# Scores of two heads as a pair, joint sums, a third unit in float32, and weights on another queue

## The chip, the cores and the metric

The kernel runs on one core of a Trainium2 chip. The metric is the device time of one execution in microseconds. A kernel's time is the median of its runs. The trace is one execution recorded by the hardware profiler; its span runs from the first to the last instruction.

## The reference

Attention over 4 batches, 8 heads, 768 positions and head size 64, with a mask that keeps the first `n_sink` = 4 keys and the last `window` = 128 keys of each row; its output, as 3072 rows of 512, goes through a feed-forward layer of 2048 hidden columns. All in float32:

```python
scores = scale * np.matmul(q, k.transpose(0, 1, 3, 2))
keep = is_sink | in_window
scores = np.where(keep, scores, -1000000000.0)
scores = scores - np.max(scores, axis=-1, keepdims=True)
a = np.exp(scores)
a = a / (np.sum(a, axis=-1, keepdims=True) + 1e-09)
x = np.matmul(a, v)                 # heads side by side: [3072, 512]
h = x @ w_in                        # [512, 2048]
g = h * np.clip(h + 3.0, 0.0, 6.0) / 6.0
out = g @ w_out                     # [2048, 512]
```

## The kernel before

**Tiling.** The queries of a batch are cut into three units of 256 rows (u = 0, 1, 2). A unit holds four pairs of heads. The 48 pairs are numbered s: first the units u = 0 of the four batches (s = 0 to 15), then the others (s = 16 to 47). A pair needs, for each head h and each half t of 128 query rows, a block of scores of 128 or 256 keys (u = 0) or 272 (u above 0), the sinks included.

**Two arithmetics.** A float32 number is either used as it is, in a matmul on float32 operands which the trace shows as two records, or split into a rounded part and a remainder of type float32r, whose products are summed in PSUM. Which way a pair goes is decided by `plain(s)` (line 223): pairs s < NF32 with u = 0 are plain float32 (NF32 = 8, the first two units). A plain pair keeps its head's 64 rows of q and k where they were loaded (rows 0 to 63 for head 0, 64 to 127 for head 1) and scores with 64 rows (L306). A split pair goes through `B_k` and `B_q`: ScalarE makes the rounded half and VectorE the remainder (`split_parts`, L29 and L35), and eight transfers on SyncE's queue (L261, L274) lay them out as 128 rows `K` and `Q`. It also splits v (`A_v`), the transposed probabilities (`D_pt`: `ph`, `pl`), and joins two halves of its result (`E_out`: `tmp`).

**Stages of a pair.** `A_v` and `A_kq` load; `B_k`, `B_q` split and lay out; `C_score` multiplies and VectorE adds the mask and takes the extremum (L313); `C_soft` runs exp with sums on ScalarE (L335), two small VectorE instructions on the sums of one head (L337, L338), and the scaling of the blocks (`norm`, L321 or L323); `D_pt` transposes on TensorE; `E_av` multiplies by v; `E_out` writes the unit's input of the feed-forward layer.

**Order.** A loop over s issues the stages of three pairs by the string `ORDER` (line 548): C of pair s-1, E of s-2, loads of s+1, B of s, D of s-1. Each `-` is a `drain`, which issues one step of the feed-forward work in hand: half of an `ffn1` block (12 matmuls, L451) or an `ffn2` of one half (6 matmuls, L471). A unit has 34 such steps. A drain issues nothing while the weights of its step have not been issued. What is left after the last loop is drained at the end. `keep_busy` puts float32 matmuls without use (L81) on TensorE in the first loops.

**Weights.** They come as 64-bit numbers in 32 parts of 512 KB. `load_part` (L148) transfers a part into a buffer (`st`, three of them; each fourth part uses `vs`), ScalarE and VectorE turn it into float32 with two instructions each (L153, L157, L159, L161) and then split it with one each (L35, L164). `W` in the loop issues one part in loops 1 to 4 and four in loops 5 to 11 (`WN`). The transfer is issued by GpSimd. A buffer is free again when the fourth instruction has read it. All other transfers in the loops are issued by SyncE's queue, which waits in order.

The instructions of an engine stand in the order that the framework gave them when it scheduled the program by dependencies and buffers; it can differ a little from the order of the source.

Of the kernel before, what the change touches and what calls it, by code (L numbers as in the profile page):

```python
# [18 lines left out]
P = 128  # L19
SK = 16  # L20
WMAX = 128
SCALE = 0.125
BIG = 1.0e30
WARM = (10, 16, 4)
# [20 lines left out]
def attn_ffn_kernel(ctx: ExitStack, tc: tile.TileContext, qx, kx, vx, vfx, vsx, n_sink, window, w_in, w_out, out):  # L45
    nc = tc.nc
    B, NU, NP = qx.shape[0:3]
    NT, DM = out.shape
    NFP = w_in.shape[0]
    H, D, UT = 2 * NP, 64, 256  # L50
    S = NU * UT
# [5 lines left out]
    work = fast.enter_context(tc.tile_pool(name="work", bufs=2))  # L57
    ps = fast.enter_context(tc.tile_pool(name="ps", bufs=8, space=PSUM))
# [75 lines left out]
    def load_part(hi, lo, src, rows, at):  # L134

        def like(t):
            return t.rearrange("p (a b) -> p a b", a=rows)

        if not wide:
            st = like(work.tile([P, 512], F32, tag="st", name="st", bufs=3))  # L140
            nc.sync.dma_start(out=st, in_=src)
            split_parts(nc, hi, lo, st, nc.scalar, nc.vector)
            return

        tag, bufs = ("vs", 1) if at % 4 == 3 else ("st", 3)
        st = work.tile([P, 512, 2], I32, tag=tag, name="st", bufs=bufs)
        it = work.tile([P, 512], I32, tag="wt", name="wt", bufs=3)
        nc.gpsimd.dma_start(out=like(st.rearrange("p n w -> p (n w)")), in_=src.bitcast(I32))  # L148
        low, high = st[:, :, 0], st[:, :, 1]
        ft = it.bitcast(F32)  # L150


        nc.scalar.activation(out=ft, in_=high.bitcast(F32), func=AF.Abs, scale=2.0 ** -112)  # L153

        nc.scalar.activation(out=low, in_=low.bitcast(U32), func=AF.Copy, scale=2.0 ** -29 * (1 - 2.0 ** -18),  # L157
                             bias=7.5 * 2.0 ** -18 - 0.5)
        nc.vector.scalar_tensor_tensor(out=low, in0=high, scalar=-2 ** 31, in1=low,  # L159
                                       op0=ALU.bitwise_and, op1=ALU.bitwise_or)  # L160
# [56 lines left out]

    NF32 = 8  # L220
    PFE = "AA"
    XHF = "A"

    def plain(s):
        return s < NF32 and pus[s][1] == 0

# [59 lines left out]
    def cell(s, h, t, c0, c1):  # L286

        if plain(s):
            return st_[s][f"P{h}"][:, t * P + c0:t * P + c1]
        return st_[s]["P"][:, h, t, c0:c1]  # L290

    def C_score(s, h, t):
        b, u, p = pus[s]
        d = st_[s]
        i = 2 * h + t
        if i == 0:
            if not plain(s):
                d["P"] = work.tile([P, 2, 2, WP], F32, name="Pt", bufs=1)
            d["nb"], d["sm"], d["rc"] = (work.tile([P, 4], F32, name=x, bufs=3) for x in ("nb", "sm", "rc"))
        if t == 0 and plain(s):  # L300
            tag, bufs = PTAGS[(2 * s + h) % len(PTAGS)]
            d[f"P{h}"] = work.tile([P, 3 * P], F32, tag=tag, name="Ph", bufs=bufs)
        k0c, w, m = spans(u)[t]
        sp = ps.tile([P, 512], F32, tag="bank", name="sp")
        if plain(s):
            nc.tensor.matmul(out=sp[:, 0:w], lhsT=d["qr"][D * h:D * (h + 1), t * P:(t + 1) * P],  # L306
                             rhs=d["kr"][D * h:D * (h + 1), k0c:k0c + w], start=True, stop=True)
        else:
            K, Q = d["K"], d["Q"]
            for part in range(2):  # L310
                nc.tensor.matmul(out=sp[:, 0:w], lhsT=Q[:, h, t * P:(t + 1) * P],  # L311
                                 rhs=K[:, h, part, k0c:k0c + w], start=(part == 0), stop=(part == 1))
        d["min"] = nc.vector.tensor_tensor_reduce(out=cell(s, h, t, 0, w), in0=sp[:, 0:w], in1=m[:, 0:w], scale=-SCALE,  # L313
                                       scalar=3.0e38, op0=ALU.add, op1=ALU.min,
                                       accum_out=d["nb"][:, i:i + 1])

    NORM0, NORM = "DADA", "AAAA"

    def norm(e, blk, c):
        if e == "A":  # L320
            nc.scalar.mul(out=blk, in_=blk, mul=c)  # L321
        elif e == "D":
            nc.vector.tensor_scalar(out=blk, in0=blk, scalar1=c, scalar2=None, op0=ALU.mult)  # L323
        else:
            nc.gpsimd.tensor_scalar(out=blk, in0=blk, scalar1=c, scalar2=1.0, op0=ALU.mult, op1=ALU.mult)

    def C_soft(s, h):
        b, u, p = pus[s]
        d = st_[s]
        nb, sm, rc = d["nb"], d["sm"], d["rc"]  # L330
        hs = slice(2 * h, 2 * h + 2)
        live = [(0, W2), (0, W2)] if u else [(0, P), (0, 2 * P)]
        for t in range(2):
            i, blk = 2 * h + t, cell(s, h, t, *live[t])
            d["exp"] = nc.scalar.activation(out=blk, in_=blk, func=AF.Exp, scale=-1.0,  # L335
                                            bias=nb[:, i:i + 1], accum_out=sm[:, i:i + 1])
        nc.vector.tensor_scalar(out=sm[:, hs], in0=sm[:, hs], scalar1=1e-9, scalar2=None, op0=ALU.add)  # L337
        nc.vector.reciprocal(out=rc[:, hs], in_=sm[:, hs])  # L338
        for t in range(2):
            i, blk = 2 * h + t, cell(s, h, t, *live[t])  # L340
            norm((NORM0 if s < START else NORM)[i], blk, rc[:, i:i + 1])
        if u and h == 1:

            ss = ssc[:, :, 0:4 * SK].rearrange("p t (k h y) -> p t k h y", k=2, h=2)
            snk_in = d["P"].rearrange("p h t w -> p h (t w)")[:, :, 2 * P:2 * WP].rearrange(
                "p h (t y) -> p t h y", t=2)[:, :, :, 0:SK]
            split_parts(nc, ss[:, :, 0], ss[:, :, 1], snk_in, weng(SSE, 0), weng(SSE, 1))
# [178 lines left out]
    B_k(0)  # L526
    B_q(0)

    def slot_C(s, h, t):
        if 0 <= s < NS:  # L530
            C_score(s, h, t)
            if t == 1:
                C_soft(s, h)
                if s == 0 and h == 1:
                    keep_busy(WARM[1])
                elif 0 < s < NP:
                    keep_busy(WARM[2])

    def slot_E(s, h):
        if 0 <= s < NS:  # L540
            E_av(s, h)
# [3 lines left out]
                dsts = [out[r0 + P * tt:r0 + P * (tt + 1), :] for tt in range(2)]  # L545
                queues.append(ffn_steps(units.index((b, u)), xt[(b, u)], work, ps, ps, dsts, "bank"))

    ORDER = "V C00 - C01 E0 - C10 - C11 E1 L - Bk - Bq W - D0 - S D1 -"
    MULT = [1] * 12
    WN = [0, 1, 1, 1, 1, 4, 4, 4, 4, 4, 4, 4]  # L550

    for s in range(NS + 2):
        if s == 3:
            later_constants()
        for step in ORDER.split():
            if step == "-":
                drain(MULT[s] if s < len(MULT) else 1)
            elif step[0] == "C":
                slot_C(s - 1, int(step[1]), int(step[2]))
            elif step[0] == "E":  # L560
                slot_E(s - 2, int(step[1]))
            elif step == "V":
                if s < NS:
                    A_v(s)
                if 2 <= s and pus[s - 2][1:] == (1, 0):
                    batch_loads(pus[s - 2][0])
            elif step == "L" and s + 1 < NS and s > 0:
                A_kq(s + 1)
            elif step == "Bk" and 0 < s < NS:
                B_k(s)  # L570
            elif step == "Bq" and 0 < s < NS:
                B_q(s)
            elif step == "W":
                for _ in range(WN[s] if s < len(WN) else 0):
                    with ExitStack() as behind:
                        if s <= 5:
                            at = max(min(s, NP) - 2, 0)
                            behind.enter_context(tc.issue_after(st_[at]["min"].ins))
                            behind.enter_context(tc.issue_after(st_[at]["exp"].ins))
                        w_order.pop(0)()  # L580
            elif step[0] == "D" and 0 <= s - 1 < NS:
                D_pt(s - 1, int(step[1]))
            elif step == "S" and 0 <= s - 1 < NS:
                D_snk(s - 1)
# [169 lines left out]
```

## Time and profile before

| What | Value |
|---|---|
| Time, median of 3 runs | 763.09 us |
| The three runs | 757.99, 763.09, 764.73 us |
| Profiled execution: span | 757.9 us |
| Profiled execution: its time outside the span | not told by the page |
| TensorE busy | 727.6 us (96%) |
| VectorE busy | 504.2 us (67%) |
| ScalarE busy | 455.8 us (60%) |
| GpSimd busy | 21.1 us (3%) |

How to read it: matmuls of one stream overlap in the records, so TensorE's busy time says where it had work, and the distance from the start of one record to the start of the next says what a matmul costs in the stream. Busy shares are means over the span, and the span has stages: the first loops have no feed-forward work, the next ones load the weights, the others do not.

### The profile page before, as it was taken

The numbers are of one execution on the slowest core, as the hardware profiler recorded it, in microseconds if no ns is written. First come the engines' busy times: TensorE is split into PE (matmuls) and PEld (weight loads), VectorE is DVE, ScalarE is ACT, GpSimd is POOL, SyncE is SP. The second block draws the span as 40 slices with busy tenths as digits, with TensorE's granted clock in tenths as the row PEclk, the third lists the DMA queues.
The fourth block names the chain that finished last, engine by engine and source line by source line (L and its number), as shares of the span: only waits on it lengthen the run. The fifth ranks groups of instructions, "written<-read, shape, count | busy, mean of one in ns | idle before, by whom it ended". The sixth has DMA issues, their size and how long they took to land.

```text
span 757.9 us, 14097 instructions
## 1 busy us (share of the span) xinstructions
PE 727.6 (96%) x4932; PEld 657.7 (87%) x4932; DVE 504.2 (67%) x1434; ACT 455.8 (60%) x1115; POOL 21.1 (3%) x49
## 2 busy tenths in 40 slices
PE   8899788799999999999999999999999999999996
PEld 7676677699989999999999899899999989999895
DVE  4788898866767767776767676766776676532321
ACT  4898987666666656666755765755765764411111
POOL 3011111000000000000000000000000000000000
PEclk9999999999999999999999999999999999999999
DMA  5556856335455455454553554554554542000000
GB/s 193 164 186 199 270 168 204 96 91 135 117 137 138 108 135 140 111 133 110 143 130 98 140 134 112 136 128 105 142 135 105 134 114 60 29 1 1 29 1 32
DMA packets 57134, 89.88 MB, mean 119 GB/s; under 512 B 8672, under 2 KB 40416, under 8 KB 57056
## 3 DMA queue, kind: packets, MB, share of 16 engines
q1 hardware_dynamic: 52304, 72.12, 36.2%
q0 software_dynamic: 4608, 16.78, 6.8%
q8 instruction: 41, 0.67, 0.4%
q14 instruction: 37, 0.30, 0.1%
q10 hardware_dynamic: 144, 0.00, 0.0%
HBM read 41.68 MB, written 6.29 MB: 63 GB/s over the span
## 4 chain that ended last, share of the span: by engine, by line
PE 75%; DVE 9%; ACT 7%; DMA 5%; issue 3%; SPq 0%; DVEq 0%; ACTq 0%; POOLq 0%
PE hps L451 29%; PE o L471 29%; PE av L413 6%; PE sp L311 4%; PE pt L355 4%; DMA st<-in_w_in_dram 2%; PE sp L306 1%; ACT Pt L335 1%; PE idle L81 1%; ACT Pt L321 1%; DVE wt L161 1%; DVE st L159 1%; DMA Q<-qt 1%; DVE gf L458 1%; DVE tmp L435 1%
## 5 line engine op out<-in xcount | busy, mean ns | idle before, releaser
L451 PE MATMUL hps<-xh,wih 128*128 128x256 f32 x768 | 220.1, 287 | 5.8 <-ACT wih L35 5.2
L451 PE MATMUL hps<-xh,wil 128*128 128x256 f32 x768 | 217.0, 283 | 0.1
L451 PE MATMUL hps<-xl,wih 128*128 128x256 f32 x768 | 216.3, 282 | 0.0
L471 PE MATMUL o<-woh,gh 128*128 128x512 f32 x384 | 155.2, 404 | 6.3 <-DVE gh L41 3.2
L451 PEld LDWEIGHTS hps<-xh,wih 128*128 128x128 f32 x768 | 144.8, 189 | 10.0 <-ACT wih L35 7.7
L471 PE MATMUL o<-woh,g 128*128 128x512 f32 x384 | 151.8, 396 | 0.0
L471 PE MATMUL o<-wol,gh 128*128 128x512 f32 x384 | 151.1, 394 | 0.0
L451 PEld LDWEIGHTS hps<-xl,wih 128*128 128x128 f32 x768 | 144.6, 188 | 1.4
L451 PEld LDWEIGHTS hps<-xh,wil 128*128 128x128 f32 x768 | 144.5, 188 | 0.8 <-DVE wil L164 0.3
L335 ACT ACTIVATE Pt<-Pt,nb 128x272 f32<-128x272 f32 (+2 forms) x160 | 81.0, 506 | 70.8 <-DVE nb L313 68.9
L457 ACT ACTIVATE gf<-hps,three 128x512 f32<-128x512 f32 x96 | 65.9, 686 | 89.4 <-PE hps L451 88.7
L458 DVE SCALAR_TENSOR_TENSOR gf<-gf,hps 128x512 f32<-128x512 f32 x96 | 66.0, 687 | 68.3 <-ACT gf L457 66.9
L313 DVE CUSTOM_DVE_ANT_0 Pt<-sp,m_t 128x272 f32<-128x272 f32 x128 | 56.0, 439 | 54.6 <-PE sp L311 53.8
L321 ACT ACTIVATE Pt<-Pt,rc 128x272 f32<-128x272 f32 (+2 forms) x158 | 72.1, 503 | 26.5 <-DVE rc L338 24.3
L471 PEld LDWEIGHTS o<-woh,g 128*128 128x128 f32 x384 | 72.1, 188 | 18.0 <-DVE g L460 1.6
L471 PEld LDWEIGHTS o<-woh,gh 128*128 128x128 f32 x384 | 72.4, 189 | 17.6 <-DVE gh L41 4.9
L471 PEld LDWEIGHTS o<-wol,gh 128*128 128x128 f32 x384 | 72.5, 189 | 10.6
L35 ACT ACTIVATE ph<-pt 128x512 fp32r<-128x512 f32 (+1 forms) x80 | 46.1, 580 | 39.1 <-PE pt L355 38.0
L311 PE MATMUL sp<-K,Q 128*128 128x272 f32 (+2 forms) x320 | 64.3, 286 | 5.3 <-DMA Q<-qt 3.2
L30 DVE TENSOR_TENSOR pl<-pt,ph 128x512 fp32r<-128x512 f32 (+1 forms) x80 | 52.7, 661 | 24.1 <-ACT ph L35 23.2
L460 DVE TENSOR_TENSOR g<-gf,gh 128x512 fp32r<-128x512 f32 x96 | 66.2, 690 | 1.1
L311 PEld LDWEIGHTS sp<-K,Q 128*128 128x128 f32 x320 | 53.7, 188 | 12.7 <-issue 2.1
(95 smaller groups left out, 968.5 us busy)
## 6 DMA issues: line engine op xcount, KB each, us to landing
K<-kt SPq DMA_DIRECT2D x128, 200.0 KB, 3.3
Q<-qt SPq DMA_DIRECT2D x160, 64.0 KB, 2.4
st<-in_w_in_dram POOLq DMA_DIRECT2D x16, 512.0 KB, 4.7
st<-in_w_out_dram POOLq DMA_DIRECT2D x16, 512.0 KB, 5.1
kr<-in_kx_dram SPq DMA_DIRECT2D x32, 200.0 KB, 2.5
qr<-in_qx_dram SPq DMA_DIRECT2D x48, 128.0 KB, 2.1
out_dram<-ost SPq DMA_DIRECT2D x24, 256.0 KB, 2.4
vr<-in_vx_dram SPq DMA_DIRECT2D x32, 192.0 KB, 2.6
```

What stands on the lines that cost most here:

```text
L30: lo_engine.tensor_tensor(out=lo, in0=src, in1=hi.bitcast(F32), op=ALU.subtract)
L35: nc.scalar.mul(out=out, in_=src, mul=scale)
L311: nc.tensor.matmul(out=sp[:, 0:w], lhsT=Q[:, h, t * P:(t + 1) * P], rhs=K[:, h, part, k0c:k0c + w], start=(part == 0), stop=(part == 1))
L313: d["min"] = nc.vector.tensor_tensor_reduce(out=cell(s, h, t, 0, w), in0=sp[:, 0:w], in1=m[:, 0:w], scale=-SCALE, scalar=3.0e38, op0=ALU.a ...
L321: nc.scalar.mul(out=blk, in_=blk, mul=c)
L335: d["exp"] = nc.scalar.activation(out=blk, in_=blk, func=AF.Exp, scale=-1.0, bias=nb[:, i:i + 1], accum_out=sm[:, i:i + 1])
L413: nc.tensor.matmul(out=o, lhsT=l, rhs=r, start=(j == 0 and (h == 0 or not plain(s))), stop=(j == len(seq) - 1 and (h == 1 or not plain(s))))
L451: nc.tensor.matmul(out=hp[:, half, :], lhsT=l, rhs=r, start=(j == 0), stop=(j == n - 1))
L457: nc.scalar.activation(out=gf, in_=hp, func=AF.Relu, bias=three, scale=1.0)
L458: nc.vector.scalar_tensor_tensor(out=gf, in0=gf, scalar=6.0, in1=hp, op0=ALU.min, op1=ALU.mult)
L460: eng(GLO, state["n"] * NP).tensor_tensor(out=g, in0=gf, in1=gh.bitcast(F32), op=ALU.subtract)
L471: nc.tensor.matmul(out=acc, lhsT=l[:, f, ts_], rhs=r[i][:, f, :], start=(i == 0 and f == 0 and j == 0), stop=(i == NFP - 1 and f == 1 and ...
```

## The change

Four edits. The transfer of a weight part is issued by SyncE's queue in place of GpSimd's. NF32 goes from 8 to 12, so the third unit (s = 8 to 11) is plain float32. In a plain pair all four score blocks are issued in one step, for each half t the two heads one behind the other; split pairs score one head per step. `C_soft` becomes `C_exp` (the four exps, then one sum and one reciprocal for four columns in place of two for two) and `C_norm` (the four scalings and the sinks' split), each a step of its own in `ORDER`. The number of drains in a loop stays eight.

```diff
-        nc.gpsimd.dma_start(out=like(st.rearrange("p n w -> p (n w)")), in_=src.bitcast(I32))
+        nc.sync.dma_start(out=like(st.rearrange("p n w -> p (n w)")), in_=src.bitcast(I32))
...
-    NF32 = 8
+    NF32 = 12
...
-    def C_score(s, h, t):
+    def C_score(s, h):
...
+        elif plain(s):
+            return
+        heads = range(2) if plain(s) else (h,)
+        for t, (k0c, w, m) in enumerate(spans(u)):
+            ts, ks = slice(t * P, (t + 1) * P), slice(k0c, k0c + w)
+            sp = {g: ps.tile([P, 512], F32, tag="bank", name="sp") for g in heads}
+            for g in heads:
+                if plain(s):
+                    gs = slice(D * g, D * (g + 1))
+                    nc.tensor.matmul(out=sp[g][:, 0:w], lhsT=d["qr"][gs, ts], rhs=d["kr"][gs, ks],
+                                     start=True, stop=True)
+                else:
+                    for part in range(2):
+                        nc.tensor.matmul(out=sp[g][:, 0:w], lhsT=d["Q"][:, g, ts], rhs=d["K"][:, g, part, ks],
+                                         start=(part == 0), stop=(part == 1))
+            for g in heads:
+                i = 2 * g + t
...
+                d["min"] = nc.vector.tensor_tensor_reduce(out=cell(s, g, t, 0, w), in0=sp[g][:, 0:w], in1=m[:, 0:w],
+                                                          scale=-SCALE, scalar=3.0e38, op0=ALU.add, op1=ALU.min,
+                                                          accum_out=d["nb"][:, i:i + 1])
...
-    def C_soft(s, h):
...
+    def C_exp(s):
         d = st_[s]
...
+        for i in range(4):
+            blk = cell(s, i // 2, i % 2, *live(s)[i % 2])
             d["exp"] = nc.scalar.activation(out=blk, in_=blk, func=AF.Exp, scale=-1.0,
...
-        nc.vector.tensor_scalar(out=sm[:, hs], in0=sm[:, hs], scalar1=1e-9, scalar2=None, op0=ALU.add)
-        nc.vector.reciprocal(out=rc[:, hs], in_=sm[:, hs])
...
+        nc.vector.tensor_scalar(out=d["sm"], in0=d["sm"], scalar1=1e-9, scalar2=None, op0=ALU.add)
+        nc.vector.reciprocal(out=d["rc"], in_=d["sm"])
+
+    def C_norm(s):
+        u = pus[s][1]
+        d = st_[s]
+        for i in range(4):
+            blk = cell(s, i // 2, i % 2, *live(s)[i % 2])
+            norm((NORM0 if s < START else NORM)[i], blk, d["rc"][:, i:i + 1])
+        if u:
...
-    ORDER = "V C00 - C01 E0 - C10 - C11 E1 L - Bk - Bq W - D0 - S D1 -"
+    ORDER = "V C0 - C1 E0 X - E1 L - N - Bk - Bq W - D0 - S D1 -"
...
+                    if step[0] == "C":
+                        C_score(s - 1, int(step[1]))
+                    else:
+                        {"X": C_exp, "N": C_norm}[step](s - 1)
+                    if step == "X" and s - 1 < NP:
+                        keep_busy(2 * WARM[2] if s > 1 else WARM[1])
```

## Rows read from the trace of the kernel before

**Rows 1.** busy time by stretch; columns: stretch, length, busy PE, PEld, DVE, ACT, POOL

```profile
...
40.00:80.00 40.00, 36.50 (x211) 28.78 (x210) 34.43 (x97) 35.27 (x89) 5.83 (x11) 1.00 0.65 202
...
85.00:152.00 67.00, 56.05 (x371) 48.92 (x368) 58.03 (x151) 51.60 (x125) 6.55 (x12) 1.00 0.60 176
160.00:740.00 580.00, 577.68 (x4038) 531.97 (x4037) 374.78 (x1058) 330.45 (x805) 0.00 (x0) 1.00 0.40 104
...
```

**Rows 2.** waits of TensorE, in us: total, times, longest

```profile
...
PE hps L451 <- ACT wih L35: 5.2, 5, 1.5
...
PE sp L311 <- DVE gf L458: 1.4, 1, 1.4
...
```

**Rows 3.** timeline of TensorE, first pairs; columns: start, length, what, count

```profile
...
1.13 4.63 PE L81 MATMUL idle<-rel 128*128 128x128 f32 x20 [1.13 <-POOL rel L65]
6.98 1.66 PE L306 MATMUL sp<-kr,qr 64*128 64x128 f32 x8 [1.21 <-DMA qr<-in_qx_dram]
...
15.32 0.92 PE L306 MATMUL sp<-kr,qr 64*128 64x128 f32 x4
16.17 1.16 PE L81 MATMUL idle<-rel 128*128 128x128 f32 x8
17.17 0.82 PE L413 MATMUL av<-pf,VF 128*128 128x256 f32 x4
17.91 0.92 PE L306 MATMUL sp<-kr,qr 64*128 64x128 f32 x4
...
```

**Rows 4.** timeline of TensorE around one split pair with u = 0

```profile
...
163.61 0.34 PE L311 MATMUL sp<-K,Q 128*128 128x128 f32 x2
163.78 0.44 PE L471 MATMUL o<-woh,gh 128*128 128x512 f32 x1
...
165.21 0.40 PE L311 MATMUL sp<-K,Q 128*128 128x256 f32 x2
165.45 0.34 PE L413 MATMUL av<-ph,VS 128*128 128x256 f32 x2
...
165.85 0.29 PE L451 MATMUL hps<-xh,wih 128*128 128x256 f32 x1
...
```

**Rows 5.** VectorE's groups by shape; busy us, mean ns of one, idle before

```profile
...
L435 DVE TENSOR_TENSOR tmp<-av,tmp 64x256 f32<-64x256 f32 x80 | 33.5, 419 | 13.6 <-ACT tmp L434 12.3
...
L337 DVE TENSOR_SCALAR sm<-sm 128x2 f32<-128x2 f32 x96 | 16.1, 168 | 29.7 <-ACT Pt L335 27.7 <-ACT Ph L335 1.6
...
L41 DVE CAST xh<-tmp 128x256 fp32r<-128x256 f32 x40 | 11.7, 291 | 5.6 <-PE hps L451 4.9
...
L30 DVE TENSOR_TENSOR pl<-pt,ph 128x384 fp32r<-128x384 f32 x16 | 8.8, 553 | 0.4
...
L30 DVE TENSOR_TENSOR kt<-kr,kt 128x256 fp32r<-128x256 f32 x8 | 3.4, 421 | 0.8 <-ACT kt L35 0.8
...
```

**Rows 6.** ScalarE's groups by shape, same columns

```profile
...
L335 ACT ACTIVATE Pt<-Pt,nb 128x272 f32<-128x272 f32 x128 | 66.7, 521 | 61.9 <-DVE nb L313 60.1
...
L434 ACT COPY tmp<-av 64x256 f32<-64x256 f32 x80 | 29.4, 368 | 17.6 <-DVE tmp L435 9.4 <-DVE xl L437 6.8
...
L35 ACT ACTIVATE kt<-kr 128x256 fp32r<-128x256 f32 x8 | 3.3, 418 | 1.1 <-DMA K<-kt 0.8 <-DMA Q<-qt 0.2
...
L35 ACT ACTIVATE xh<-av 128x256 fp32r<-128x256 f32 x8 | 2.9, 367 | 0.5 <-PE av L413 0.4
...
```

**Rows 7.** DMA issues: count, KB each, median us from issue to landing

```profile
...
st<-in_w_in_dram POOLq DMA_DIRECT2D x16, 512.0 KB, 4.7
...
VF<-in_vfx_dram SPq DMA_DIRECT2D x8, 256.0 KB, 3.8
...
```

**Rows 8.** chain of waits, 45 to 165 us: start, length, what

```profile
...
60.23 5.58 DMA st<-in_w_out_dram
...
118.14 4.72 DMA st<-in_w_in_dram
...
```

**Rows 9.** waits of SyncE's queue: total, times, longest

```profile
...
SPq L231 <- PE sp L306: 54.2, 8, 12.7
...
```

More of the change, by code (lines that the diff above doesn't have):

```diff
@@ L290, in cell @@
         return st_[s]["P"][:, h, t, c0:c1]
-    def C_score(s, h, t):
+    def C_score(s, h):
         b, u, p = pus[s]
         d = st_[s]
-        i = 2 * h + t
-        if i == 0:
+        if h == 0:
+            d["nb"], d["sm"], d["rc"] = (work.tile([P, 4], F32, name=x, bufs=3) for x in ("nb", "sm", "rc"))
             if not plain(s):
                 d["P"] = work.tile([P, 2, 2, WP], F32, name="Pt", bufs=1)
[L299 to L315, printed above, removed]
@@ new lines, in C_score @@
+        elif plain(s):
[15 more added lines that the diff above has]
+                i = 2 * g + t
+                if t == 0 and plain(s):
+                    tag, bufs = PTAGS[(2 * s + g) % len(PTAGS)]
+                    d[f"P{g}"] = work.tile([P, 3 * P], F32, tag=tag, name="Ph", bufs=bufs)
+                d["min"] = nc.vector.tensor_tensor_reduce(out=cell(s, g, t, 0, w), in0=sp[g][:, 0:w], in1=m[:, 0:w],
+                                                          scale=-SCALE, scalar=3.0e38, op0=ALU.add, op1=ALU.min,
+                                                          accum_out=d["nb"][:, i:i + 1])
@@ L325, in norm, with live @@
             nc.gpsimd.tensor_scalar(out=blk, in0=blk, scalar1=c, scalar2=1.0, op0=ALU.mult, op1=ALU.mult)
-    def C_soft(s, h):
-        b, u, p = pus[s]
+    def live(s):
+        return [(0, W2), (0, W2)] if pus[s][1] else [(0, P), (0, 2 * P)]
+    def C_exp(s):
         d = st_[s]
[L330 to L334, printed above, removed]
-            d["exp"] = nc.scalar.activation(out=blk, in_=blk, func=AF.Exp, scale=-1.0,
-                                            bias=nb[:, i:i + 1], accum_out=sm[:, i:i + 1])
-        nc.vector.tensor_scalar(out=sm[:, hs], in0=sm[:, hs], scalar1=1e-9, scalar2=None, op0=ALU.add)
-        nc.vector.reciprocal(out=rc[:, hs], in_=sm[:, hs])
[L339 to L342, printed above, removed]
+        for i in range(4):
+            blk = cell(s, i // 2, i % 2, *live(s)[i % 2])
+            d["exp"] = nc.scalar.activation(out=blk, in_=blk, func=AF.Exp, scale=-1.0,
+                                            bias=d["nb"][:, i:i + 1], accum_out=d["sm"][:, i:i + 1])
+        nc.vector.tensor_scalar(out=d["sm"], in0=d["sm"], scalar1=1e-9, scalar2=None, op0=ALU.add)
[7 more added lines that the diff above has]
+        if u:
             ss = ssc[:, :, 0:4 * SK].rearrange("p t (k h y) -> p t k h y", k=2, h=2)
@@ L527, in attn_ffn_kernel @@
     B_q(0)
[L529 to L537, printed above, removed]
     def slot_E(s, h):
@@ L557, in attn_ffn_kernel @@
                 drain(MULT[s] if s < len(MULT) else 1)
-            elif step[0] == "C":
-                slot_C(s - 1, int(step[1]), int(step[2]))
+            elif step in ("C0", "C1", "X", "N"):
+                if 0 <= s - 1 < NS:
+                    if step[0] == "C":
[4 more added lines that the diff above has]
+                        keep_busy(2 * WARM[2] if s > 1 else WARM[1])
             elif step[0] == "E":
```

## The prediction

> **What bounds the kernel now.** I read the busy time by stretch first. From 160 to 740 us TensorE is busy for 577.68 of 580.00 us [rows 1]: nothing is left to gain there but its own work, which the change does not touch for the 32 pairs with u above 0. From 85 to 152 us, where weights are loaded and pairs 8 to 12 pass, it has work for 56.05 of 67.00 us, while VectorE is busy for 58.03 and ScalarE for 51.60. From 40 to 80 us it misses 3.5 of 40 us, with VectorE at 34.43 and ScalarE at 35.27. All feed-forward work must pass TensorE whenever its turn comes, so the time is TensorE's work plus its idle time. A microsecond counts if it leaves one of the two.
>
> Next, who ends TensorE's waits: most often the rounding of a weight part on ScalarE, 5.2 us in 5 waits [rows 2]. Then the chain of waits: between 45 and 165 us it runs through VectorE, ScalarE and four whole landings of weight parts, the first of 5.58 us at 60.23, the last of 4.72 us at 118.14 [rows 8]. That stretch is set by making weights beside the split pairs; the matmuls only follow.
>
> **The change, part by part.** The profiled execution has a span of 757.9 us. What lies around it is not told; the fastest of the three runs is 757.99, the median 763.09, 5.2 above the span. I make the sum against the span and carry the difference over to the median.
>
> *Scores of two heads side by side.* Pair 0 already had all four blocks in one stretch: eight records in 1.66 us [rows 3]. Its neighbours were slow then (20 useless matmuls in 4.63 us, 0.23 each, against 8 in 1.16 us, 0.14 each, later). Scaled by that, the eight would take 1.0 us later, while the next pair needs 0.85 us for one head (15.32 to 16.17) and 0.92 for the other. So the two heads do run beside each other, and I take 0.85 us for both: 0.85 saved per pair. The ends are no saving (eight records at the 1.66 us they took) and 0.85. Pairs 1 to 3, in front of all feed-forward work, give 3 x 0.85 = 2.5 us. For pairs 4 to 7 the 3.4 us lie where VectorE and ScalarE set the pace, and I count 1 us; the rest becomes a wait.
>
> *Third unit in float32: TensorE.* Transposes are the same. A plain pair costs 0.85 for scores and 2 x 0.74 for the products with v (17.17 to 17.91) [rows 3], 2.33 us. A split pair costs 0.17 + 0.24 for one head's scores (163.61 to 163.78, 165.21 to 165.45) and 0.40 for its products (165.45 to 165.85) [rows 4], for two heads 1.62 us. That adds 0.71 us per pair, 2.9 us for four. Without side-by-side scores it is 1.56 us per pair, 6.2 us.
>
> *Third unit: VectorE and ScalarE.* VectorE drops the remainders of k, q and v (0.42 us each; the row of k stands for three groups), two of the probabilities at 0.55, two joins at 0.42 and a copy of 0.29 [rows 5]: 1.26 + 1.11 + 0.84 + 0.29 = 3.50 us per pair, 14.0 for four. ScalarE drops three roundings at 0.42 (again one row for three) and two copies at 0.37, and takes over one at 0.37 [rows 6]: 1.6 us net per pair, 6.5 for four. Eight transfers per pair leave SyncE's queue. What it buys is the idle time of 85 to 152 us, 10.95 us. VectorE would be busy for about 58.03 - 14.0 - 1.7 (next part) = 42.3 us there, ScalarE for 45.1; over some 62 us that is 68% and 73%, near the 65% and 57% of the later stretch, in which TensorE hardly waits [rows 1]. Gone at most: all 10.95. Gone at least: nothing, if the weights' own round trip sets the pace. I take 8 us, nearer to the upper end because VectorE is the busiest engine there, and leave 3 us because a loop's first feed-forward step after the weights still needs the part just issued [rows 2]. Late next: that part.
>
> *Joint sums.* Two VectorE instructions fewer per pair, 0.17 us each (the reciprocal is like the row of the sums) [rows 5]: 0.33 us, 1.7 us over the five loops above and some 16 us in all. From 160 us on this frees an engine that no one waits for: nothing gained. The cover is VectorE's 205 us of free time there. The useless matmuls stay as many as before.
>
> *Steps of C in a new order.* Scores of split pairs end two drains earlier, so K and Q are free earlier: good for their transfers, worth at most the 2.3 us that TensorE misses after 160 us; I take 0. The scaling now stands three drains ahead of the transposes; see rival three.
>
> *Weights on SyncE's queue.* 32 issues move. Ahead of them in the queue now stand the loads of k and q, which wait for scores to free their buffers: 54.2 us in 8 waits, 6.8 on average, up to 12.7 [rows 9]. Behind them stand the loads of pairs used a loop or more later, which can wait. With the third unit plain, no K and Q transfers are left in that queue until the weights are through. A 512 KB part lands in 4.7 us from GpSimd's queue, a 256 KB load in 3.8 us from SyncE's [rows 7]; between a few tenths less and 6.8 us more per loop, I take 0, because buffers of weights come free before the scores that the loads wait for. The Trainium skill gives a first-byte latency of about 1 us on the gpsimd path and 0.6 us on the sync path (DMA: Bandwidth & Descriptors, Specifications); as an estimate from that page, 0.4 us on each of the four landings in the chain would make the sum 1.6 us lower. No row here shows a weight part from SyncE's queue.
>
> *Sum:* -2.5 - 1 + 2.9 - 8 = -8.6, about -9 us: 749 us of span, 754 us against the median.
>
> **The rivals.**
> One, no change: the weights' round trip (landing, ScalarE, VectorE) sets 85 to 152 us, not the sum of work. For it: the four landings in the chain [rows 8]. Against it: VectorE at 87%. The idle time stays, the dearer matmuls and the saved scores vanish in it: -2.5 - 1 = -3.5, 759.6 us. That side-by-side scores bring nothing at full pace belongs here too.
>
> Two, no change: banks. A plain pair now takes four PSUM banks at once where a step took one, beside those of two units of feed-forward work; TensorE then waits for VectorE, as it did once for 1.4 us for a result of the feed-forward [rows 2]. In each of the eight pairs 4 to 11 that is 11 us: +2, 765 us. Against it: one such wait in the whole trace. The Trainium skill has row tiling raise the pressure on PSUM, since each tile writes its own bank (TensorEngine Tiling (Array Packing), Gotcha 1: PSUM Pressure); by that rule this rival is what would happen, and the trace has it in one place only.
>
> Three, slower: in the 32 loops of u above 0 the first exp waits until all scores of the pair are issued. If the transposes then come before the scaling, TensorE waits 0.5 us (one exp, 0.52 [rows 6]) per loop: +16 - 9 = +7, 770 us. It decides when the way from scores to scaling is longer than five drains of 1.43 us (163.78 to 165.21 [rows 4]), 7.2 us. Against it: four exps are 2.1 us.
>
> Four, slower: a weight part stands behind a load that waits for scores. In loops 7 to 11 the landings lie on the chain, so the average wait of 6.8 us [rows 9] would count in five loops: +34 - 9 = +25, 788 us. It decides at (9 + 7.6) / 5 = 3.3 us per loop. Against it: the order above.
>
> Five, more gain: all 10.95 us and the 3.5 of 40 to 80 go, with 2.5 at the start, against 2.9: -14, 749 us.
>
> **The numbers.** What a measurement of this kernel tells from no change is about 1%, 7.6 us (the runs shown spread by 6.7). Chances: forecast 0.50 (own range -16 to -4, 747 to 759), one 0.16, two 0.06, three 0.09, four 0.09, five 0.10. Two thirds of the forecast and all of five are faster by over 1%: 0.34 + 0.10 = 0.44. The other third, one and two are within: 0.16 + 0.16 + 0.06 = 0.38. Three and four are slower: 0.18. The range runs from 742 (five, with the landings shorter and all of the 3.4 us of pairs 4 to 7) to 769 (half of three), and leaves out four and the worse half of three.
>
> **What would show it.** Right: TensorE busy for all but 3 or 4 us of the stretch in which weights load, VectorE near 68% there, four plain score blocks in under 1 us. Wrong: landings of weights still whole on the chain; scores waiting for banks; transposes waiting for ScalarE's scaling after 160 us; SyncE's queue holding a weight part for a wait on scores.

## The result and the profile after

The changed kernel takes 749.36 us (median of 4 runs, 748.57 to 751.12); the kernel before, with a fourth run beside the changed kernel's, 761.61 us (757.99 to 764.73). The ratio is 0.9851 (95% interval 0.9816 to 0.9885), so 12 us faster. The forecast was 754 us, the range 742 to 769. In the runs after, the time is the span plus 1.8 us; the profiled execution has a span of 749.3 us and a time of 751.12. Span against span it is 757.9 - 749.3 = 8.6 us, to the tenth the sum of the prediction. It will turn out that almost none of its terms was right.

First the busy time by stretch of the changed kernel (stretch, length, then busy time and instructions of PE, PEld, DVE, ACT and POOL, TensorE's granted clock, DMA share, GB/s), which answers to [rows 1]:

```profile
...
40.00:80.00 40.00, 35.35 (x206) 28.53 (x205) 36.64 (x94) 36.47 (x86) 0.00 (x0) 0.96 0.67 215
85.00:152.00 67.00, 65.31 (x396) 55.46 (x395) 47.01 (x118) 46.42 (x116) 0.95 (x1) 0.97 0.44 131
...
300.00:640.00 340.00, 335.39 (x2360) 306.12 (x2360) 222.85 (x628) 211.65 (x527) 0.00 (x0) 1.00 0.45 116
160.00:740.00 580.00, 574.90 (x3985) 524.98 (x3984) 357.37 (x967) 320.29 (x783) 0.00 (x0) 1.00 0.39 101
...
```

The stretch of 85 to 152 us looks just as forecast: TensorE idle for 1.69 us where it was 10.95, VectorE at 47.01 of 67 us (70%; "near 68%" was said). But from 160 us on TensorE misses 5.1 us where it missed 2.3. Between 300 and 640 us alone it is busy for 335.39 us; before it was

```profile
...
300.00:640.00 340.00, 338.05 (x2409) 312.32 (x2408) 237.07 (x685) 219.68 (x539) 0.00 (x0) 1.00 0.48 123
...
```

Who ends TensorE's waits after (total, times, longest), against [rows 2]:

```profile
...
PE hps L461 <- ACT wih L35: 3.3, 4, 1.4
PE o L481 <- DVE rc L344: 2.3, 1, 2.3
...
PE pt L365 <- DVE Ph L330: 1.2, 2, 0.8
...
PE sp L309 <- ACT pf L35: 0.8, 1, 0.8
...
```

The wait for a rounded weight part (5.2 us before) is 3.3. Transposes wait for the scaling only at the start (1.2 us, both times before 17 us); before it was

```profile
...
PE pt L355 <- DVE Ph L323: 2.5, 3, 1.1
...
```

The timeline of TensorE at the start, against [rows 3]:

```profile
...
5.80 0.93 PE L309 MATMUL sp<-kr,qr 64*128 64x128 f32 x8
6.66 3.84 PE L81 MATMUL idle<-rel 128*128 128x128 f32 x32
...
12.26 0.93 PE L309 MATMUL sp<-kr,qr 64*128 64x128 f32 x8
13.11 0.92 PE L423 MATMUL av<-pf,VF 128*128 128x256 f32 x4
...
```

Eight records of a plain pair's scores give way to the next work after 0.86 and 0.85 us, as taken (0.85). Groups of VectorE by shape (busy us, mean ns of one, idle before), against [rows 5]: fewer split products, and one sum and one reciprocal for four columns, each as long as those for two.

```profile
...
L445 DVE TENSOR_TENSOR tmp<-av,tmp 64x256 f32<-64x256 f32 x72 | 30.2, 419 | 13.7 <-ACT tmp L444 12.9
...
L344 DVE RECIPROCAL rc<-sm 128x4 f32<-128x4 f32 x48 | 8.5, 177 | 1.4
L343 DVE TENSOR_SCALAR sm<-sm 128x4 f32<-128x4 f32 x48 | 8.2, 170 | 33.1 <-ACT Pt L341 28.5 <-ACT Ph L341 4.5
...
```

ScalarE's exps, against [rows 6], are as long as before (521 ns then):

```profile
...
L341 ACT ACTIVATE Pt<-Pt,nb 128x272 f32<-128x272 f32 x128 | 66.1, 517 | 52.3 <-DVE nb L320 50.8
...
```

The weights' issues (KB each, median us from issue to landing), against [rows 7], and the landings that stand in the chain of waits (start, length) between 38 and 150 us, against [rows 8]:

```profile
...
st<-in_w_in_dram SPq DMA_DIRECT2D x16, 512.0 KB, 4.0
st<-in_w_out_dram SPq DMA_DIRECT2D x16, 512.0 KB, 5.0
...
```

```profile
...
38.15 3.79 DMA st<-in_w_in_dram
...
42.94 4.94 DMA st<-in_w_out_dram
...
88.08 3.75 DMA st<-in_w_in_dram
...
102.18 4.21 DMA st<-in_w_in_dram
...
```

Landings still stand whole on the chain; the last begins 16 us earlier than the last of before (118.14). The waits in SyncE's queue, against [rows 9]:

```profile
...
SPq L148 <- DVE wt L161: 42.5, 21, 4.0
...
SPq L231 <- PE sp L309: 18.3, 8, 5.8
...
```

A weight part waits there for its own buffer (42.5 us in 21 waits); the loads that wait for scores do so for 18.3 us where it was 54.2. While such a load waits, the weight parts behind it wait too. VectorE's L161 has freed a buffer at 51.84 us (50.55 and 1.29), but the next part of `w_out` is issued at 54.01, behind a load of k that the scores release:

```profile
...
50.55 1.29 DVE L161 SCALAR_TENSOR_TENSOR wt<-wt,st 128x512 int32<-128x512 int32 x2
...
```

```profile
...
53.09 0.33 SPq L231 DMA_DIRECT2D kr<-in_kx_dram  x1
53.47 0.42 SPq L232 DMA_DIRECT2D qr<-in_qx_dram  x1
54.01 1.09 SPq L148 DMA_DIRECT2D st<-in_w_out_dram  x2
...
```

That part is held for 2.17 us, another for 2.56 (63.53 to 66.08), four more for 0.6 to 0.9.

**A ledger.** The clearest comparison is when the first score of a pair is issued. These are starts of score records read from the traces of five kernels (experiments below), us from the span's start:

| Pair | before | before, SyncE's queue | changed, GpSimd's queue | changed | changed, steps as before |
|---|---|---|---|---|---|
| 0 | 7.0 | 6.0 | 7.0 | 5.8 | 6.2 |
| 4 | 38.5 | 33.7 | 30.2 | 28.9 | 30.2 |
| 8 | 85.1 | 81.8 | 80.2 | 75.3 | 75.9 |
| 12 | 151.8 | 145.5 | 143.8 | 136.5 | 135.1 |
| 14 | 177.3 | 170.3 | 171.7 | 164.4 | 164.4 |
| 24 | 313.5 | 306.5 | 308.8 | 301.3 | 300.2 |
| 47 | 640.5 | 633.6 | 640.9 | 633.7 | 628.9 |
| span | 757.9 | 750.8 | 757.0 | 749.3 | 743.3 |

Read the changed kernel against before by differences: 9.7 us are won up to pair 4, 0.2 from there to pair 8, 3.0 from pair 8 to 14 (5.4 up to pair 12, 2.4 of them lost again) and then, with nothing in the change that should matter any more, 5.4 us are lost between pair 24 and pair 47 (327.0 us before, 332.4 after). Both the gain and the loss needed a cause. Each column is one execution. A second trace of the changed kernel, below, has pair 4 at 28.9 us and 332.2 us from pair 24 to 47, as here, but pair 12 at 139.3 and pair 14 at 167.1, so between pairs 4 and 24 a difference under 3 us can be chance.

### The profile page after: what moved, and what is told of

Read it like the earlier page. It is cut to its first block, busy times and chain, and to the rows that moved or that the text cites. A ratio compares the mean times of both kernels' runs of the same rounds, so it can differ in the third digit from the quotient of the medians.

```text
span 749.3 us, 13811 instructions
## 1 busy us (share of the span) xinstructions
PE 727.1 (97%) x4932; PEld 653.4 (87%) x4932; DVE 477.9 (64%) x1306; ACT 445.9 (60%) x1099; POOL 4.0 (1%) x17
## 4 chain that ended last, share of the span: by engine, by line
PE 69%; ACT 12%; DVE 10%; DMA 5%; issue 2%; SPq 1%; ACTq 0%; DVEq 0%
PE o L481 28%; PE hps L461 27%; PE av L423 5%; PE pt L365 4%; PE sp L313 3%; ACT Pt L328 2%; ACT Pt L341 2%; DMA st<-in_w_in_dram 2%; ACT Ph L341 1%; DVE gf L468 1%; DVE g L470 1%; ACT gf L467 1%; DMA K<-kt 1%; DVE Pt L320 1%; ACT st L157 1%
## 5 line engine op out<-in xcount | busy, mean ns | idle before, releaser
L341 ACT ACTIVATE Pt<-Pt,nb 128x272 f32<-128x272 f32 (+2 forms) x144 | 73.4, 510 | 59.9 <-DVE nb L320 58.5
L328 ACT ACTIVATE Pt<-Pt,rc 128x272 f32<-128x272 f32 (+2 forms) x144 | 66.0, 506 | 18.4 <-DVE rc L344 18.3
L470 DVE TENSOR_TENSOR g<-gf,gh 128x512 fp32r<-128x512 f32 x96 | 66.1, 689 | 1.4
L320 DVE CUSTOM_DVE_ANT_0 Pt<-sp,m_t 128x272 f32<-128x272 f32 x128 | 52.3, 438 | 20.7 <-PE sp L313 19.9
L30 DVE TENSOR_TENSOR pl<-pt,ph 128x512 fp32r<-128x512 f32 (+1 forms) x72 | 48.4, 674 | 16.8 <-ACT ph L35 16.3
L35 ACT ACTIVATE ph<-pt 128x512 fp32r<-128x512 f32 (+1 forms) x72 | 42.1, 585 | 19.5 <-PE pt L365 17.2
L313 PE MATMUL sp<-K,Q 128*128 128x272 f32 (+2 forms) x288 | 47.3, 288 | 0.4 <-DMA Q<-qt 0.4
L313 PEld LDWEIGHTS sp<-K,Q 128*128 128x128 f32 x288 | 42.2, 189 | 3.6 <-DMA Q<-qt 0.6
```

The costliest lines, as they stand in the source:

```text
L30: lo_engine.tensor_tensor(out=lo, in0=src, in1=hi.bitcast(F32), op=ALU.subtract)
L35: nc.scalar.mul(out=out, in_=src, mul=scale)
L313: nc.tensor.matmul(out=sp[g][:, 0:w], lhsT=d["Q"][:, g, ts], rhs=d["K"][:, g, part, ks], start=(part == 0), stop=(part == 1))
L320: d["min"] = nc.vector.tensor_tensor_reduce(out=cell(s, g, t, 0, w), in0=sp[g][:, 0:w], in1=m[:, 0:w], scale=-SCALE, scalar=3.0e38, op0=AL ...
L470: eng(GLO, state["n"] * NP).tensor_tensor(out=g, in0=gf, in1=gh.bitcast(F32), op=ALU.subtract)
```

## The experiments

Every run stands beside runs of the kernel before on the same chip (761.46 to 761.69 us, medians of 13).

**Which part is it?** Four kernels undo one part each.

Weights on GpSimd's queue again:

```diff
-        nc.sync.dma_start(out=like(st.rearrange("p n w -> p (n w)")), in_=src.bitcast(I32))
+        nc.gpsimd.dma_start(out=like(st.rearrange("p n w -> p (n w)")), in_=src.bitcast(I32))
```

> The changed kernel (749.4 us) with the weight parts issued by GpSimd's queue again, the rest as changed. Theory A (the prediction's: the queue move is worth nothing): 749 to 751 us, pair 4's first scores at about 29 us as in the changed kernel. Theory B (the queue move carries part of the gain at the start, since weight transfers stand in front of the first loads of q and k): first scores at 7.0 us instead of 5.8, the higher clock later, pair 4's scores at 31 us or later, 752 us or more.

Measured: 759.76 us (10 runs, 754.79 to 762.48), ratio to before 0.9974 (0.9944 to 1.0003). The whole gain is gone, a larger loss than either theory had, though the matmuls, the third unit and the order are those of the changed kernel. Its stretches:

```profile
...
40.00:80.00 40.00, 33.84 (x183) 26.82 (x181) 33.30 (x86) 32.91 (x78) 6.34 (x12) 0.91 0.58 193
85.00:152.00 67.00, 63.47 (x385) 53.86 (x384) 48.53 (x123) 48.62 (x121) 5.18 (x9) 0.97 0.48 143
...
```

TensorE misses 3.53 us in 85 to 152 us, 7.4 less than before, and the kernel is no faster: the idle time of a fixed stretch says little once other work stands in it. By the ledger this kernel is 1.3 us behind the changed one at pair 4, 4.9 at pair 8, 7.3 at pair 12, and keeps those 7.3.

The third unit split again:

```diff
-    NF32 = 12
+    NF32 = 8
```

> The changed kernel with only two units in plain float32 (NF32 = 8), the rest as changed. Theory A (VectorE's relief by the third unit is the larger term): 5 us slower than the changed kernel, 754 to 755 us, TensorE's missing time between pairs 8 and 14 up by 8 us. Theory B (the gain came before the feed-forward work starts): 749 to 751 us, since pairs 0 to 7 stay as changed.

Measured: 749.92 us (749.21 to 750.53), 0.9862 (0.9811 to 0.9913). The third unit, the largest term of the sum, is worth nothing that can be told (the changed kernel has 749.36 here and 751.90 in its second series). In 85 to 152 us VectorE is busy for 57.52 of 67 us again (86%) and TensorE misses 4.35, and it costs no time. In the trace pairs 8 and 12 come 2 us later, and pair 14 comes 1.2 us earlier, no more than two traces of one kernel differ.

The second head's scores of a plain pair after E0, one drain later (`P` is the step that issues them; the lines of the loop that call it are left out):

```diff
-        heads = range(2) if plain(s) else (h,)
+        heads = (h,)
...
-    ORDER = "V C0 - C1 E0 X - E1 L - N - Bk - Bq W - D0 - S D1 -"
+    ORDER = "V C0 - C1 E0 P X - E1 L - N - Bk - Bq W - D0 - S D1 -"
```

> The changed kernel, but a plain pair's second head is scored behind the products of the pair before (E0), not beside the first head; joint exps and sums stay. Theory A: 0.85 us per pair where nothing hides it, pairs 1 to 3 and part of the others: 752 to 753 us, pair 4's first scores at 31.5 us. Theory B (the start was won by the order of exps and scaling, not by scores side by side): 749 to 750 us, pair 4's scores at 29 to 30 us.

Measured: 751.36 us (750.88 to 751.86), 0.9883 (0.9833 to 0.9934); pair 4 at 30.3 us in place of 28.9. Side by side is worth 1.4 us at the start, where both traces of the changed kernel have 28.9. In all it is 2.0 us against the first series of the changed kernel and nothing against the second (751.90); the sum had 3.5.

Split pairs with the old steps (`C00` to `C11`, sums of one head, scaling beside the exps), plain pairs as changed (the functions of the old steps are left out):

```diff
+    ORDER1 = "V C00 - C01 E0 - C10 - C11 E1 L - Bk - Bq W - D0 - S D1 -"
...
-        for step in ORDER.split():
+        for step in (ORDER1 if 0 <= s - 1 < NS and not plain(s - 1) else ORDER).split():
```

> The changed kernel, but the 36 split pairs keep the steps of the kernel before (one score block per step, exps, sums and scaling head by head); plain pairs as changed. Theory A (the new order costs nothing after 160 us): 749 to 750 us. Theory B (the new order makes the feed-forward wait for VectorE after 160 us, some 4 us of the 5.2 that TensorE misses there): 745 to 746 us, TensorE's missing time from 160 to 740 us back from 5.1 to about 2.3 us.

Measured: 750.62 us (749.72 to 754.80), 0.9887 (0.9828 to 0.9946). From pair 24 to 47 it takes 332.0 us: what is lost after 160 us stays lost. The new order of exps and scalings isn't the cause.

**The queue alone.** The kernel before, with nothing but the queue moved:

```diff
-        nc.gpsimd.dma_start(out=like(st.rearrange("p n w -> p (n w)")), in_=src.bitcast(I32))
+        nc.sync.dma_start(out=like(st.rearrange("p n w -> p (n w)")), in_=src.bitcast(I32))
```

> The kernel before with one edit, the weight parts issued by SyncE's queue. Theory R (the round trip of the weight buffers, from free to landed to free, sets the loops in which weights load, and GpSimd's queue makes each of its seven generations about 1 us longer): 6 to 9 us faster than before, 753 to 756 us. Theory S (the move only brings the first loads forward): 1 to 2 us faster, 760 us. The rival of the prediction (a part stands behind a load that waits for scores): slower than before, the more so as its K and Q transfers for pairs 8 to 11 are in the same queue.

Measured: 751.39 us (750.08 to 752.61), 0.9862 (0.9818 to 0.9906). So the queue alone takes 10.2 us off, and putting it back costs the changed kernel 10.4. In the ledger it is 4.8 us by pair 4 and 7.0 by pair 14, and stays 7; the rest of the 10.2 is that the profiled execution before was a fast one of its kernel (about 1.9 us below the median) and this one the slowest of four.

Of the 4.8 us by pair 4 only 1.0 is the earlier first score (7.0 to 6.0). The rest goes with TensorE's pace in these two executions. Before, the eight records of the first scores take 1.66 us and the 32 useless matmuls behind them 6.17; with SyncE's queue it is 0.93 and 3.84. Before also has a stretch at the lower clock from 23.7 to 27.1 us (0.50, 1.2 of 2.4 GHz), after TensorE had been idle for 1.08 us up to 21.98; the other has none before pair 4. The 32 matmuls, and the clock (0.63) over 4.6 us around that stretch:

```profile
...
8.56 6.17 PE L81 MATMUL idle<-rel 128*128 128x128 f32 x32
...
```

```profile
...
23.10:27.70 4.60, 4.60 (x18) 3.68 (x18) 1.99 (x6) 2.29 (x7) 0.53 (x1) 0.63 0.36 119
...
```

The changed kernel on GpSimd's queue has its first score at 7.0 us as well, and yet the 32 matmuls in 3.84 us, so there the queue is worth 1.3 us by pair 4 and not 4.8.

**Where in the loading?** The changed kernel, the first four parts on SyncE's queue, the other 28 on GpSimd's:

```diff
-        nc.sync.dma_start(out=like(st.rearrange("p n w -> p (n w)")), in_=src.bitcast(I32))
+        (nc.sync if at < 4 else nc.gpsimd).dma_start(out=like(st.rearrange("p n w -> p (n w)")), in_=src.bitcast(I32))
```

> The changed kernel with the first four weight parts issued by SyncE's queue and the other 28 by GpSimd's. Theory R: nearly all of the loss that all 32 on GpSimd's queue gave comes back, 757 to 759 us, with pair 4's scores at 29 us as in the changed kernel and pair 9's at 93 us or later. Theory S: 749 to 751 us.

Measured: 760.37 us (10 runs, 756.68 to 764.84), 0.9991 (0.9958 to 1.0024). Pair 4 comes at 28.9 us, as in the changed kernel; the time is lost later, with the 28 parts. Pair 9 comes at 91.2 us, 2.3 later than in the changed kernel but not at 93; the profiled execution was the fastest of the ten, with a span of 754.9.

The timelines show one leg of the way. A part can be issued when the last reader of its buffer (L161, VectorE) is done. With GpSimd's queue, VectorE's L161 (start, length) and the next issue:

```profile
...
57.16 0.68 DVE L161 SCALAR_TENSOR_TENSOR wt<-wt,st 128x512 int32<-128x512 int32 x1
...
```

```profile
...
58.50 0.53 POOL L148 DMA_DIRECT2D st<-in_w_out_dram  x1 [2.78 <-ACT woh L35]
...
```

and in the changed kernel

```profile
...
57.85 0.69 DVE L161 SCALAR_TENSOR_TENSOR wt<-wt,st 128x512 int32<-128x512 int32 x1
...
```

```profile
...
58.61 0.33 SPq L148 DMA_DIRECT2D st<-in_w_in_dram  x1
```

From the end of L161 to the issue it is 0.66 us on GpSimd (57.84 to 58.50; the releaser is inferred, and a rounding that ends near it is named here) and 0.07 on SyncE (58.54 to 58.61). Over parts 8 to 31 (counted from 0) I took the medians of the two legs from the traces, and then means:

| Kernel | freed to issue, us | issue to landing, us | freed to issue, mean | whole round trip, mean | last remainder of a weight ends, us |
|---|---|---|---|---|---|
| before | 0.66 | 4.72 | 0.68 | 15.2 | 138.9 |
| before, SyncE's queue | 0.07 | 4.81 | 0.64 | 15.0 | 133.7 |
| changed, GpSimd's queue | 0.66 | 4.61 | 0.67 | 13.7 | 129.0 |
| changed | 0.07 | 4.21 | 0.37 | 12.5 | 122.1 |

The parts behind the first four go through seven generations of the four buffers, and 7 us lie between the last two rows, so that 1 us for each generation would do. The medians of the two legs give it (0.59 and 0.40), but they leave out the parts that SyncE's queue holds: six of 24 in the changed kernel, eight in the kernel before on SyncE's queue (up to 3.24 us, behind transfers of Q and k). By the means of the whole round trip (freed, issued, landed, freed again) the changed kernel wins 1.1 us per generation, 0.3 of it up to the issue, 0.4 up to the landing and 0.4 from the landing until ScalarE and VectorE are done. In the kernel before it wins 0.2, and 4.8 of the 5.2 us between the first two rows stand there when the first eight parts are through (47.5 against 42.7 us). The trace on SyncE's queue has two stretches at the lower clock (0.5, at 47.0 and 81.1 us) that the one before has not, which may hide a part. So the move of the queue is the cause of the gain, but 0.6 us in every generation is not shown to be the way.

**Is it this round trip?** Two tests. A small transfer into the same buffer ahead of each part, which has to land first:

```diff
+        nc.sync.dma_start(out=like(st.rearrange("p n w -> p (n w)"))[:, 0:1, 0:128], in_=src.bitcast(I32)[:, 0:1, 0:128])
         nc.sync.dma_start(out=like(st.rearrange("p n w -> p (n w)")), in_=src.bitcast(I32))
```

> The changed kernel with a small transfer into the same buffer ahead of each weight part, on which the part's transfer must wait: a round trip longer by one landing, some 2 us. Theory R (the round trip of the weight buffers sets the loops 5 to 11): about 2 us for each of seven generations, 8 to 14 us slower than the changed kernel, 757 to 763 us, with more stretches at the lower clock. The prediction's view (work on ScalarE and VectorE sets them, the landing is covered): 749 to 752 us.

Measured: 758.43 us (10 runs, 756.92 to 763.87), 0.9978 (0.9942 to 1.0013): 6.5 us more than the changed kernel beside it (751.90), 9.1 more than that kernel at first. A longer trip on the same queue gives most of the gain back. But it does not count in full: from freed to issue it is now 3.63 us (median) in place of 0.07, which would be 25 us in seven generations. From landing to freed a part takes 6.5 us (mean) in place of 7.7, so ScalarE and VectorE take up some of it. Nor is it the round trip alone: SyncE's queue waits for the small transfers, and the loads behind them with it (pair 4 comes at 31.6 us, not 28.9).

One buffer fewer, so that each part waits for the one before the last:

```diff
-        tag, bufs = ("vs", 1) if at % 4 == 3 else ("st", 3)
+        tag, bufs = ("vs", 1) if at % 4 == 3 else ("st", 2)
```

> The changed kernel with two buffers for weight parts in place of three (the outputs, which share them, have two as well). Theory R: with fewer parts in flight the round trip counts more often, 8 us or more slower, 757 us or more. If the work on ScalarE and VectorE sets those loops (the prediction): 749 to 752 us.

Measured: 753.49 us (751.18 to 754.36), 0.9899 (0.9854 to 0.9943). Slower, but by 1.6 to 4.1 us only, less than the theory of the round trip wants. With two buffers a part is also worked off faster: from ScalarE's first instruction on it to L161's end it takes 4.4 us (median) against 6.8 with three, so part of the trip with three buffers is queueing on ScalarE and VectorE, which shrinks when fewer parts wait at once. A buffer more was not tried. The two tests say that the round trip counts, and that much of a longer one is taken up; why the small delay on GpSimd's queue costs as much as it does stays open.

**The loss after 160 us.** The number of drains per loop is the same, but a drain is empty while the weights of its step have not been issued. Counted from the records, 53 feed-forward steps lie ahead of pair 13's scores in the kernel before and 54 in the changed one: one drain more found work. All later loops are shifted by that step. Which edit does it is open: 53 stands with the queue alone, 54 in each of the kernels that undo one part. If the shift is the cause, adding steps mends it. Three extra drains in loop 13:

```diff
+        if s == 13:
+            drain(3)
```

> The changed kernel with three more feed-forward steps issued once, in loop 13, so that the sequence of steps in the later loops stands as in the kernel before (there 53 steps before pair 13, in the changed kernel 54). Theory P (after 160 us the changed kernel loses some 4 us because an ffn2 step now follows its ffn1 too closely): 745 to 746 us, TensorE's missing time from 160 to 740 us at 2 to 3 us. Theory O (the new order of exps costs them): 749 to 750 us, missing time as in the changed kernel, 5.1 us.

Measured: 748.53 us (746.93 to 749.43), 0.9834 (0.9790 to 0.9877), which is not the 745 to 746 of theory P: 0.8 us under the first series of the changed kernel, 3.4 under the second. But pair 24 to 47 takes 326.7 us, as in the kernel before, and TensorE is busy in 300 to 640 us for

```profile
...
300.00:640.00 340.00, 337.92 (x2396) 311.93 (x2395) 225.40 (x637) 213.00 (x532) 0.00 (x0) 1.00 0.46 117
...
```

The cheapest shift, by drains at the start of loop 14 until the number of steps issued is 1 above a multiple of four:

```diff
+                    done[0] += 1
...
+        if s == 14:
+            while done[0] % 4 != 1:
+                drain(1)
```

> The changed kernel with feed-forward steps added at the start of loop 14 until their count stands there, modulo four, as in the kernel before. Theory P: 1 to 3 us faster than the changed kernel in the same job, TensorE's missing time between 300 and 640 us back from 4.6 to about 2 us. Theory O (the new order of exps costs it): no difference.

Measured: 744.05 us (743.56 to 745.07), 0.9775 (0.9707 to 0.9843), faster than both kernels, by more than theory P had (7.9 us under the changed kernel beside it, 5.3 under its first series). TensorE misses 3.4 us between 300 and 640 us, not 2. Of steps with matmuls 55 lie ahead of pair 13's scores in place of 54 (`done` also counts the two that write out a unit). The expectation is wrong in one point: modulo four, 55 does not stand as the 53 of the kernel before; the 57 of the kernel above do. TensorE's waits in 300 to 640 us, first of the changed kernel, then of this one:

```profile
...
PE o L481 <- DVE gh L41: 2.0, 5, 0.9
PE av L423 <- DVE vs L30: 0.9, 3, 0.4
PE o L481 <- DVE g L470: 0.9, 1, 0.9
PE sp L313 <- DMA Q<-qt: 0.4, 1, 0.4
```

```profile
...
PE o L481 <- DVE gh L41: 2.1, 2, 1.1
PE spt L384 <- DVE ssc L30: 0.9, 1, 0.9
```

With the shift, `ffn2` comes so close behind its `ffn1` that it waits for VectorE's activation of it (L41, L470), five times and once. From pair 24 to 47 this kernel takes 328.7 us for the same 174 steps; that is 3.7 us less than the changed kernel, so the rest of what its median wins lies elsewhere or is noise.

More weights earlier, with the same mending:

```diff
-    WN = [0, 1, 1, 1, 1, 4, 4, 4, 4, 4, 4, 4]
+    WN = [0, 2, 2, 2, 2, 4, 4, 4, 4, 4, 4, 0]
```

> The changed kernel with two weight parts in each of loops 1 to 4 and none in loop 11, and the steps of the later loops in the order of the kernel before. Theory R: the weights are through one loop earlier and the loops that wait for them are fewer, 744 to 747 us. Rival: the first loops, with ScalarE busy for 32.5 of 40 us, become longer by what is saved later, 748 to 750 us.

Measured: 746.49 us (745.75 to 747.51), 0.9813 (0.9744 to 0.9882): in theory R's range, but 2.4 us slower than the one above, which has the same mending. Pair 4 comes at 33.8 us in place of 30.2; what the weights win later (65 steps at pair 14, not 63) they cost at the start.

The changed kernel once more, beside these three:

> The changed kernel itself, for a comparison on the same chip: 748.5 to 751 us by every theory.

Measured: 751.90 us (748.68 to 754.13), 0.9870 (0.9794 to 0.9945).

All fourteen traces agree on the shift: with 54 steps ahead of pair 13's scores (nine traces) pair 24 to 47 takes 332.0 to 332.6 us; with 53 (two) 327.0 each, with 55, 57 and 59 (one each) 328.7, 326.7 and 325.3.

## Why the prediction came out

The time lay in the range, and the span difference equals the sum. That is chance: by its own steps,

- **Weights on SyncE's queue, taken as 0** (between a few tenths less and 6.8 us more per loop): this step failed. It is -7 us in the profiled spans and -10 in the medians. I asked only whether SyncE's queue would hold a part back, and bounded the gain by a few tenths because the landings of [rows 7] were alike. The landing is not all: from buffer free to issue it is 0.66 us on GpSimd's queue and 0.07 on SyncE's when nothing holds the part, a leg that no row of mine showed. How much of the 7 to 10 us comes by this leg is open (round trip above); some of it is clock. My reason for the 0 argued the other way: a buffer that comes free before the scores is one whose part waits, as at 54.01. The Trainium skill says that issuing from several engines only saves the sequencer's time to start a transfer, usually small beside the transfer (DMA: Bandwidth & Descriptors, Issuing engines are not separate DMA queues). Here the issue is small beside the landing as well (0.66 against 4.72 us), and yet the move was worth 10 us. The 1.6 us that I worked out from its first-byte latencies counted four landings and was too small.
- **Third unit, +2.9 and -8:** 0 together (`NF32` back at 8: 749.92 against 749.36). VectorE did fall to 70% in 85 to 152 us, as forecast; it just wasn't what set the time there. Rival one named the weights' round trip, with 0.16, which the two tests bear out in part; its time, 759.6 us, is what came (759.76) when the queue was left as it was. "For it" stood the four landings of [rows 8], and I let VectorE's 87% outweigh them. Of the signs that were to prove the forecast wrong, "landings of weights still whole on the chain" came, and "SyncE's queue holding a weight part for a wait on scores" came in part, beside all three that were to prove it right.
- **Scores side by side, -2.5 - 1:** the 0.85 us per pair is right; in time it brings 1.4 us at the start and in all 2 us at most.
- **The start:** 9.7 us up to pair 4, not 2.5. 4.8 of it is the queue when it is moved first, most of that TensorE's pace in the one execution before, but 1.3 when it is moved last; 1.4 is the pairing. The rest (3.5 or 7.0) came with neither the third unit nor the split pairs' order (pair 4 at 28.9 us in both of those kernels). What remains is the joint sums, the new order of exps and scalings in the plain pairs and the place of the useless matmuls, which now stand together behind `X`; none was tried alone. 1.3 us of it can be seen as the transposes' shorter wait for the scaling (2.5 to 1.2).
- **Joint sums and new order, 0 from 160 us on:** a loss of about 5 us. "Nothing is left to gain there" was near the truth, but there was something to lose. Rival three had a loss there, in the wrong place: from 160 us on transposes never wait for the scaling; `ffn2` waits for VectorE, by the shift of one step. Of the 5.4 us, 2.7 are idle time of TensorE in 300 to 640 us; the rest lies in the spacing of its records. From pair 24 to 47 the distances behind matmuls of `ffn2` sum to 129.7 us for 528 records (123.8 for 522 before; six more are 1.4), those behind transposes to 19.9 (17.9), 184 each; no other kind grows by more than 0.2 us.
- **Rivals two and four:** four came, but small: two parts held for 2.17 and 2.56 us and four for 0.6 to 0.9, where it wanted 3.3 us in each of five loops; and the same move won more than that. Of waits for a PSUM bank the list has one: scores for ScalarE's copy of the transposes (`PE sp L309 <- ACT pf L35`), 0.8 us. The Trainium skill's rule that row tiles raise the pressure on PSUM (TensorEngine Tiling (Array Packing), Gotcha 1: PSUM Pressure) is borne out by no more than that.
- **The range:** its low end, 742 us, does not come out of the terms named for it: 749 less 1.6 and 3.4 is 744. Nothing hangs on it here.

In medians: the queue -10.2 us (761.6 to 751.4), all other edits with the steps set right -7.3 (to 744.05), the shifted step +5 to +8 by that kernel (to 749.4 and 751.9) and +1 to +3 by the one with three drains more (748.53); in the traces it is 3.7 to 5.7 from pair 24 to 47. Open is why GpSimd needs 0.6 us more to issue, since nothing in the trace stands in that time, and why the whole costs 7 to 10.

## What to carry to other kernels

Where a few buffers are filled, used and refilled, follow one buffer round: freed, issued, landed, read. Each leg can count once per generation, the issue too, but other legs may shrink to take it up, so change one alone and measure; a busy engine beside the ring proves nothing until then. Take means beside medians: one part in four was held, and the median hid it. When work is dealt out in steps by position, compare the sequence of steps far behind the edit: one step more or less can shift all later loops. And take one experiment that undoes the smallest edit first, even when the sum fits.

## What the runs showed of the hardware

**A stall is paid twice.** The changed kernel's TensorE stood idle for 2.33 us up to 59.02, as its timeline (start, length, what, idle before) shows:

```profile
...
59.02 0.47 PE L481 MATMUL o<-woh,gh 128*128 128x512 f32 x1 [2.33 <-DVE rc L344]
...
```

The instruction named as releaser is 0.17 us long; what the matmul reads is gh, whose rounding (L41) ended at 58.87. Then the granted clock fell; the stretch with the idle time and the next one:

```profile
...
57.00:60.40 3.40, 1.38 (x7) 1.13 (x8) 3.27 (x11) 3.40 (x11) 0.00 (x0) 0.99 0.84 285
60.40:63.80 3.40, 3.40 (x15) 2.84 (x13) 3.23 (x6) 3.40 (x8) 0.00 (x0) 0.51 0.45 151
...
```

At 0.51 it ran at 1.2 of its 2.4 GHz, so 3.4 us of work took the place of 1.7. Executions of one kernel differ with the clock as well: the 39 runs of the kernel before go from 755.74 us at a mean granted clock of 0.998 to 767.26 at 0.985. The ten runs of the changed kernel with GpSimd's queue lie between 0.987 and 0.996, the eight of the changed kernel (both series) between 0.991 and 0.999. So part of the 10 us between the medians goes with the clock; the two pairs of profiled spans have 7 to 8.
